# Nyström attention and a gated MLP on one core: the first phase's transposes, sums, landmarks, v load and w3 loads become tokens of the order string, all orders are revised, and the dummy matmuls start sooner

## The chip, the core and the metric

The kernel runs on one core of a Trainium2 chip. The metric is the device time of one execution in microseconds (us), from the first to the last of it. Most executions of one kernel agree closely on one chip; some are longer, most of these at a lower granted TensorE clock (of the kernel before on one chip, 276.58 us at 0.997 of the full clock and 284.16 at 0.978). A run is called slow when it is over 1.5% above the fastest of the same kernel, and only fast runs are compared. TensorE is called PE, VectorE DVE, ScalarE ACT, GpSimd POOL and SyncE SP in the profile.

## The reference, cut to what matters

```python
B, H, S, D = 8, 8, 576, 64          # q, k, v: fp32, 1152 KB per batch and tensor
q_lm, k_lm = means of 18 neighbouring rows of q, k        # 32 landmarks
A  = softmax(q @ k_lm.T / 8);  Bm = softmax(q_lm @ k_lm.T / 8);  C = softmax(q_lm @ k.T / 8)
Z  = Bm.T / (norm1(Bm) * norminf(Bm));  six times: Z = 2*Z - Z @ Bm @ Z
x  = A @ Z @ C @ v                                        # 4608 rows of 512
out = ((x @ w1) * (x @ w2)) @ w3 @ w_out                  # d_ff = 1024, out 4608 x 512
```

## The kernel before

The kernel folds `w3 @ w_out` into one matrix `w34` while the attention of the first batch runs. Everything is scheduled by hand: strings of one-letter tokens give the order in which pieces are issued, and each engine executes its own instructions in that order. Letters that the argument needs:

- `f`: one unit of the fold, three 512-column matmuls (0.647 us); some are preceded by four transposes of a row block of w3. There are 64 of them.
- `C`, `S`, `B`, `T`, `N`, `R`, `P`, `D`, `J`, `X`, `M`, `I`, `Z`, `G`: stages of one batch's attention. `V` multiplies by v, `A` makes scores, `D` the denominators, `I` an inverse step.
- `u`: an "up" unit of the MLP (eight matmuls, 288 columns), `d` and `db`: half of a "down" unit in one or another PSUM bank.
- `p`: a quarter of the v load of a later batch, `t`: a DMA transpose of a quarter of a later batch's q and k, `s` and `h`: GpSimd's group sums and landmarks, `w`: a load of a w3 row block.

`START` is the end of the first phase, `FIRST` the period that begins with batch 0's first `u`, then `ODD` and `EVEN` alternate, and `LAST` is batch 7.

```python
    def load_v(st, b):
        vt = st["vt"] if "vt" in st else pin.tile([128, H, 384], FP32, name="vt")
        nc.sync.dma_start(out=vt[0:NP], in_=v[b].rearrange("h (p r) d -> p h (r d)", p=NP))
        st["vt"] = vt
    # [...]
    def load_weight(t, w):             # wup: two loads of 512 KB for each of w1, w2, on GpSimd's queue
        for qd in range(2):
            nc.gpsimd.dma_start(out=wup[64 * qd:64 * qd + 64, :, t, :],
                                in_=w[256 * qd:256 * qd + 256, :].rearrange("(h d) j -> d h j", d=D))
    # [...]
    def transposes(st, t, hs):         # token t
        # [...]
        nc.sync.dma_start_transpose(out=..., in_=st["qkn"][0:NP, t, hs[0]:hs[0] + n, :]...)

    def turn_on_pe(st, t, h0, copy):   # batch 0: q and k are turned by PE instead
        # [...] 12 PE transposes into a `big` bank, then one copy to qkT

    def sums(st, t, pieces=iter(())):  # four GpSimd adds, about 4.7 us
        # [...]
    # ---- the preamble, in program order ----
        load_qk(sts[0], 0)
        load_qk(sts[1], 1)
        load_weight(0, moe_w1)
        load_weight(1, moe_w2)
        fd = fold(pw, wof, w3f, wsp, warm_up)
        # [...] 16 fold units
        w3f[4] = pf.tile([128, DF], FP32, name="w3f", bufs=3)
        nc.gpsimd.tensor_copy(out=w3f[4][0:NP, 0:1], in_=sts[0]["qkn"][0:NP, 0, 0, 0:1])   # gate: waits for q
        load_w3(4)
        sts[0]["vt"] = pin.tile([128, H, 384], FP32, name="vt")
        nc.gpsimd.tensor_copy(out=sts[0]["vt"][0:NP, 0, 0:1], in_=sts[0]["qkn"][0:NP, 1, 0, 0:1])  # gate: waits for k
        load_v(sts[0], 0)
        turn_on_pe(sts[0], 0, 0, nc.scalar.copy)
        turn_on_pe(sts[0], 0, 4, nc.vector.tensor_copy)
        sums(sts[0], 0)
        # [...] 5 f, k's two turns, w3 block 5, 2 f, landmarks, sums of k, 2 f
        load_w3(6)
        turn_all(1)                    # all four DMA transposes of batch 1, on SP's queue
        steps(fd, 5)
        run(START)
```

A gate is a one-element GpSimd copy into the tile that a load will fill. The load must wait for it, so it cannot be issued before the tensor that the gate reads has landed.

The softmax here doesn't subtract the row's maximum and nothing guards it: scores larger than these inputs give would overflow.

Of the kernel before, what the change touches and what calls it, by code (L numbers as in the profile page):

```python
# [7 lines left out]
FP32 = mybir.dt.float32  # L8
# [5 lines left out]
B = 8  # L14
# [17 lines left out]
def kernel(  # L32
# [12 lines left out]
    START = ("C0 f f h f h f S0 C1 B f w T f f N V0 f S1 A1 f A0 R D P V1 f J0 I0 p f J1 J2 "  # L45
             "I1 f f f f f f f X s I2 p f I3 f f f p I4 f M0 I5 h f s t Z M1 f h f G0 G1 t h "
             "f f G2 p h G3 p f f C0 C1 f f ")
    FIRST = ("u t t u u p S0 u p B u u V0 T A1 N u A0 P R u u f S1 u s D V1 I0 u I1 J1 I2 J0 "
             "u s u h I3 f J2 u X I4 h u u M0 d I5 M1 p Z h d t t h G0 G1 p d C0 G2 C1 G3 d ")
    EVEN = ("u t u S0 u d B p t u p T N V0 A1 u u R u s db S1 u u V1 A0 u I0 D d J0 t P I1 "  # L50
            "J1 u u I2 J2 u s X db I3 u u I4 M0 I5 t M1 u Z db h h G0 h G1 db d h C0 p d G2 "
            "G3 C1 p ")
    ODD = ("u t S0 t p u B p u A1 T N V0 d R s u u S1 u u u d A0 V1 P u I0 u D I1 u J2 s "
           "J0 d I2 u h h u p I3 J1 u u I4 d u I5 h db X db t M1 db M0 t Z db G0 G1 p C0 d "
           "G2 G3 C1 h d ")
    LAST = ("u d u u u db u u d u u db u u u u u u u u d db db db db db db db d d ")
# [474 lines left out]
    for t in qbds:  # L531
        nc.vector.memset(t, 0.0)
# [6 lines left out]
    def steps(g, n=1):  # L539
        for _ in range(n):  # L540
            next(g, None)
# [8 lines left out]
    def all_sums():  # L550
        for b in range(1, B):
            pieces = qk_pieces(sts[b + 1], b + 1) if b + 1 < B else iter(())
            for t in (0, 1):
                sums(sts[b], t, pieces=pieces)
                yield

    def all_landmarks():
        for b in range(B):
            for t in (0, 1):
                for parity in (0, 1):  # L560
                    if b or t:
                        landmarks(sts[b], t, parity)
                        yield

    def all_turns():
        for b in range(2, B):
            for t in (0, 1):
                for h0 in (0, 4):
                    transposes(sts[b], t, range(h0, h0 + 4))
                    yield  # L570

# [20 lines left out]
    queues = dict(p=loads_v(), s=all_sums(), h=all_landmarks(), t=all_turns(), u=all_ups())  # L592

    def run(names):
        for t in names.split():
# [4 lines left out]
            elif t == "w":  # L600
                load_w3(7)
# [12 lines left out]
    with tc.tile_pool(name="pf", bufs=2) as pf:  # L614
# [14 lines left out]
        nc.vector.memset(warm, 0.0)  # L629
        load_w3(0, 0)  # L630
# [16 lines left out]
        warm_up(7)  # L647
# [15 lines left out]
        w3f[4] = pf.tile([128, DF], FP32, name="w3f", bufs=3)  # L663
        nc.gpsimd.tensor_copy(out=w3f[4][0:NP, 0:1], in_=sts[0]["qkn"][0:NP, 0, 0, 0:1])
        load_w3(4)
        sts[0]["vt"] = pin.tile([128, H, 384], FP32, name="vt")
        nc.gpsimd.tensor_copy(out=sts[0]["vt"][0:NP, 0, 0:1], in_=sts[0]["qkn"][0:NP, 1, 0, 0:1])
        load_v(sts[0], 0)
        turn_on_pe(sts[0], 0, 0, nc.scalar.copy)
        turn_on_pe(sts[0], 0, 4, nc.vector.tensor_copy)  # L670
        sums(sts[0], 0)
        steps(fd, 5)
        turn_on_pe(sts[0], 1, 0, nc.scalar.copy)
        turn_on_pe(sts[0], 1, 4, nc.vector.tensor_copy)
        load_w3(5)
        steps(fd, 2)
        landmarks(sts[0], 0, 0)
        landmarks(sts[0], 0, 1)
        sums(sts[0], 1)
        steps(fd, 2)  # L680
        load_w3(6)
        turn_all(1)
        steps(fd, 5)
# [40 lines left out]
```

## Time and profile before

| | before |
|---|---|
| time, median of four runs (us) | 276.66 (275.98 to 277.29) |
| span of the profiled run (us) | 274.0, granted clock 0.999 |
| first transposes of q / first `V` / first `u` start at (us) | 19.79 / 39.90 / 69.04 |
| first period, `FIRST` (us) | 24.54 |
| one `ODD` and one `EVEN` (us) | 52.31 |

The prediction below shows the page, the chain and the waits. One more view: the DMA view of the stretch from 8 to 60 us. Its columns are the load, the issuing queue, the number of issues, the size of each and the median time from issue to landing:

```profile
wup<-in_moe_w_dram POOLq DMA_DIRECT2D x4, 512.0 KB, 30.3
vt<-in_v_dram SPq DMA_DIRECT2D x1, 1152.0 KB, 14.2
```

What matters here is that the first v load takes 14.2 us and that 2 MB of weights (as they are written, in fp16; in HBM they are 4 MB of fp32, the figure that one expectation below gives) are under way on another queue for about 30 us. The weights are issued from 14.3 us on and the last lands at 49.67; they are not needed before `G0` at 62.4 us.

### The profile page before, as it was taken

The numbers are of one execution on the slowest core, as the hardware profiler recorded it, in microseconds if no ns is written. First come the engines' busy times: TensorE is split into PE (matmuls) and PEld (weight loads), VectorE is DVE, ScalarE is ACT, GpSimd is POOL, SyncE is SP. The second block draws the span as 40 slices with busy tenths as digits, with TensorE's granted clock in tenths as the row PEclk, the third lists the DMA queues.
The fourth block names the chain that finished last, engine by engine and source line by source line (L and its number), as shares of the span: only waits on it lengthen the run. The fifth ranks groups of instructions, "written<-read, shape, count | busy, mean of one in ns | idle before, by whom it ended". The sixth has DMA issues, their size and how long they took to land.

```text
span 274.0 us, 9325 instructions
## 1 busy us (share of the span) xinstructions
PE 263.2 (96%) x3874; PEld 148.6 (54%) x3874; DVE 150.8 (55%) x380; ACT 144.0 (53%) x276; POOL 171.0 (62%) x237
## 2 busy tenths in 40 slices
PE   7999989999989999999999999999999999999993
PEld 3546555454654465456545654665465556555642
DVE  5633215464558467545865575559365655674420
ACT  4644445227625855486357455743855476435531
POOL 6446882299699979765996994779879635000000
PEclk9999999999999999999999999999999999999999
DMA  6999999999968999999899899989994231113224
GB/s 211 354 214 248 243 290 151 150 261 128 213 121 142 170 195 218 179 215 201 128 133 259 173 162 188 217 176 156 134 259 130 83 79 42 41 42 79 77 70 122
DMA packets 62138, 45.56 MB, mean 166 GB/s; under 512 B 35600, under 2 KB 54288, under 8 KB 62096
## 3 DMA queue, kind: packets, MB, share of 16 engines
q1 hardware_dynamic: 47488, 32.22, 54.3%
q0 software_dynamic: 13824, 11.54, 30.0%
q10 hardware_dynamic: 784, 1.21, 1.5%
q8 instruction: 30, 0.49, 0.8%
q14 instruction: 12, 0.10, 0.1%
HBM read 38.80 MB, written 9.44 MB: 176 GB/s over the span
## 4 chain that ended last, share of the span: by engine, by line
PE 83%; POOL 6%; DVE 3%; issue 3%; ACT 2%; DVEq 0%; POOLq 0%
PE big L428 24%; PE acc L469 12%; PE acc L508 9%; PE big L469 8%; PE big L377 6%; PE small L321 5%; PE big L411 4%; PE big L495 2%; DVE ab L434 2%; PE small L508 2%; PE big L228 2%; PE big L645 2%; PE big L293 1%; PE big L362 1%; POOL tr L193 1%
## 5 line engine op out<-in xcount | busy, mean ns | idle before, releaser
L428 PE MATMUL big<-ahat,gt 128*128 128x288 f16 x512 | 76.6, 287 | 0.8 <-ACT gt L415 0.5
L434 DVE TENSOR_TENSOR ab<-a_sb,big 128x576 f16<-128x576 f16 x64 | 48.1, 752 | 29.9 <-PE big L428 16.3
L432 ACT CAST a_sb<-big 128x576 f16<-128x576 f32 x64 | 40.8, 638 | 42.8 <-PE big L428 42.7
L428 PEld LDWEIGHTS <-gt 128*128 128x128 f16 x512 | 46.4, 100 | 18.9 <-issue 1.5
L469 PE MATMUL acc<-w,ab 128*128 128x512 f16 x184 | 47.0, 380 | 0.0
L469 PEld LDWEIGHTS <-ab 128*128 128x128 f16 x280 | 24.8, 98 | 25.5 <-issue 3.3
L508 PE MATMUL acc<-wsp,w3t 128*128 128x512 f16 x144 | 35.4, 380 | 0.0
L417 DVE TENSOR_SCALAR gt<-big 128x1024 f16<-128x1024 f32 x16 | 19.6, 1224 | 24.0 <-PE big L411 24.0
L192 POOL TENSOR_TENSOR tr<-qkT 128x768 f32<-128x768 f16 x16 | 26.2, 1637 | 7.6 <-DMA qkT<-qkn 7.5
L508 PEld LDWEIGHTS <-w3t 128*128 128x128 f16 x192 | 17.9, 98 | 18.0 <-issue 0.9
L193 POOL TENSOR_TENSOR tr<-tr,qkT 128x768 f32<-128x768 f32 x16 | 26.3, 1641 | 1.3
L236 POOL TENSOR_TENSOR t<-ect 96x384 f32<-96x384 f32 x16 | 15.9, 995 | 16.1 <-ACT ect L232 14.1
L469 PE MATMUL big<-w,ab 128*128 128x512 f16 x96 | 23.5, 380 | 0.0
L501 DVE SCALAR_TENSOR_TENSOR w3t<-big,w3t 128x512 f16<-128x512 f32 x16 | 11.0, 689 | 18.5 <-ACT w3t L500 18.5
L377 PE MATMUL big<-sz,tz 32*32 32x96 f32 (+1 forms) x768 | 19.2, 248 | 1.7 <-DVE sz L384 1.4
L473 ACT ACTIVATE o_sb<-acc 128x512 f32<-128x512 f32 x23 | 13.7, 597 | 9.7 <-PE acc L469 9.3
L415 ACT ACTIVATE gt<-big 128x1024 f16<-128x1024 f32 x16 | 16.3, 1022 | 3.5 <-PE big L411 3.4
L377 PEld LDWEIGHTS big<-sz,tz 32*32 32x32 f32 x768 | 9.0, 103 | 15.5 <-issue 10.7
L411 PE MATMUL big<-wup,zt 64*32 64x512 f16 x512 | 17.1, 379 | 0.0
L211 ACT COPY far<-o 64x256 f32<-64x256 f32 x32 | 12.9, 403 | 7.9 <-POOL o L197 7.1
L382 DVE TENSOR_TENSOR tz<-big,eye 128x64 f32<-128x64 f32 x40 | 8.8, 221 | 12.7 <-PE big L377 12.2
L500 ACT ACTIVATE w3t<-big 128x512 f16<-128x512 f32 x16 | 9.5, 596 | 11.5 <-PE big L495 11.4
(105 smaller groups left out, 373.4 us busy)
## 6 DMA issues: line engine op xcount, KB each, us to landing
vt<-in_v_dram SPq DMA_DIRECT2D x28, 288.0 KB, 4.5
out_dram<-o_sb SPq DMA_DIRECT2D x23, 192.0 KB, 2.7
qkn<-in_q_dram POOLq DMA_DIRECT2D x12, 288.0 KB, 5.1
qkn<-in_k_dram POOLq DMA_DIRECT2D x12, 288.0 KB, 6.5
w3f<-in_moe_w_dram SPq DMA_DIRECT2D x6, 512.0 KB, 6.6
out_dram<-o_sb SPq DMA_DIRECT2D x24, 128.0 KB, 3.6
wup<-in_moe_w_dram POOLq DMA_DIRECT2D x4, 512.0 KB, 30.3
out_dram<-o_sb SPq DMA_DIRECT2D x23, 64.0 KB, 2.6
```

The costliest lines, as they stand in the source:

```text
L192: nc.gpsimd.tensor_tensor(out=tr, in0=x[:, :, 0, :], in1=x[:, :, 1, :], op=ALU.add)
L193: nc.gpsimd.tensor_tensor(out=tr, in0=tr, in1=x[:, :, 2, :], op=ALU.add)
L236: nc.gpsimd.tensor_tensor(out=t3[0:NP], in0=e[:, :, 0:3, :], in1=e[:, :, 3:6, :], op=ALU.add)
L377: nc.tensor.matmul(psI[32 * t:32 * t + 32, qd, o:96], tz[sl, qd, :], sz[sl, qd, o:96], start=True, stop=True, tile_position=(32 * h, 32 * t))
L411: nc.tensor.matmul(psG[32 * h:32 * h + 32, qd, :], zt[rs, i, h, :], wup[rs, h, w, fs], start=(i == 0), stop=(i == 1), tile_position=(64 * ...
L415: nc.scalar.activation(out=g[:, :, w, fs], in_=psG, func=AXF.Copy, scale=1.0 / ZS)
L417: nc.vector.tensor_scalar(out=g[:, :, w, fs], in0=psG, scalar1=1.0 / ZS, scalar2=None, op0=ALU.mult)
L428: nc.tensor.matmul(p[:, c, 0:HS], st["g"][:, qd, w, 128 * j:128 * j + 128], st["ahat"][qd][:, c, :], start=(qd == 0), stop=(qd == 1))
L432: nc.scalar.copy(out=st["a_sb"], in_=p[:, :, 0:HS])
L434: nc.vector.tensor_tensor(out=st["ab"][:, j, st["t0"]:st["t0"] + S].rearrange("p (c s) -> p c s", c=2), in0=st["a_sb"], in1=p[:, :, 0:HS], ...
L469: nc.tensor.matmul(pso[:, :], ab[:, j, t0:t0 + 128], w34[:, j, :], start=(j == 0), stop=(j == 7))
L508: nc.tensor.matmul(psW[j][:, :], turned[j, c // 4][:, a, c % 4, :], wsp[:, b, c, :], start=(c == 0 and a + b == 0), stop=(c == 7 and a == 1))
```

## The change

It moves the rest of the first phase's hand-written sequence into `START` as tokens, with `x` (PE transposes of q and k), `v` (first v load) and `w` (w3 row blocks), so that each can stand anywhere among the fold units. The other orders are revised, and the memset of the dummy matmuls' operand goes ahead of two others so that the dummies begin sooner. The intent is fewer waits on PE.

```diff
-    START = ("C0 f f h f h f S0 C1 B f w T f f N V0 f S1 A1 f A0 R D P V1 f J0 I0 p f J1 J2 "
-             "I1 f f f f f f f X s I2 p f I3 f f f p I4 f M0 I5 h f s t Z M1 f h f G0 G1 t h "
-             "f f G2 p h G3 p f f C0 C1 f f ")
+    START = ("w x x s f v x f w x h h f f f f f f t t s f f f C0 f w f f h f f f f t S0 h p "
+             "C1 B f f T A0 V0 A1 f N S1 f t f R f D V1 w P J0 f I0 f J2 J1 f X f f f I1 s f "
+             "f I2 p f I3 f f h t I4 f p f I5 M0 f Z s h t f f G0 G1 G2 f C0 G3 h f h p M1 "
+             "C1 f f t f ")
 # [... FIRST, EVEN, ODD, LAST revised as well ...]
-    for t in qbds:
-        nc.vector.memset(t, 0.0)
 # [... sums, landmarks and DMA transposes of the first batches join their queues ...]
+    def first_v():
+        sts[0]["vt"] = pin.tile([128, H, 384], FP32, name="vt")
+        nc.gpsimd.tensor_copy(out=sts[0]["vt"][0:NP, 0, 0:1], in_=sts[0]["qkn"][0:NP, 1, 0, 0:1])
+        load_v(sts[0], 0)
+        yield
 # [... first_turns (x) and loads_w3 (w) likewise ...]
         nc.vector.memset(warm, 0.0)
+        for t in qbds:
+            nc.vector.memset(t, 0.0)
-        warm_up(7)
+        warm_up(8)
 # [... the preamble from load_w3(4) to run(START) goes, see above ...]
```

In `START` the token `s` (GpSimd's sums of q) now stands ahead of `v`, whose gate runs on GpSimd too. Two `t` stand ahead of the third `w`.

More of the change, by code (lines that the diff above doesn't have):

```diff
@@ L44 @@
     nc = tc.nc
-    START = ("C0 f f h f h f S0 C1 B f w T f f N V0 f S1 A1 f A0 R D P V1 f J0 I0 p f J1 J2 "
-             "I1 f f f f f f f X s I2 p f I3 f f f p I4 f M0 I5 h f s t Z M1 f h f G0 G1 t h "
-             "f f G2 p h G3 p f f C0 C1 f f ")
-    FIRST = ("u t t u u p S0 u p B u u V0 T A1 N u A0 P R u u f S1 u s D V1 I0 u I1 J1 I2 J0 "
-             "u s u h I3 f J2 u X I4 h u u M0 d I5 M1 p Z h d t t h G0 G1 p d C0 G2 C1 G3 d ")
-    EVEN = ("u t u S0 u d B p t u p T N V0 A1 u u R u s db S1 u u V1 A0 u I0 D d J0 t P I1 "
-            "J1 u u I2 J2 u s X db I3 u u I4 M0 I5 t M1 u Z db h h G0 h G1 db d h C0 p d G2 "
-            "G3 C1 p ")
-    ODD = ("u t S0 t p u B p u A1 T N V0 d R s u u S1 u u u d A0 V1 P u I0 u D I1 u J2 s "
-           "J0 d I2 u h h u p I3 J1 u u I4 d u I5 h db X db t M1 db M0 t Z db G0 G1 p C0 d "
-           "G2 G3 C1 h d ")
-    LAST = ("u d u u u db u u d u u db u u u u u u u u d db db db db db db db d d ")
+    START = ("w x x s f v x f w x h h f f f f f f t t s f f f C0 f w f f h f f f f t S0 h p "
+             "C1 B f f T A0 V0 A1 f N S1 f t f R f D V1 w P J0 f I0 f J2 J1 f X f f f I1 s f "
+             "f I2 p f I3 f f h t I4 f p f I5 M0 f Z s h t f f G0 G1 G2 f C0 G3 h f h p M1 "
+             "C1 f f t f ")
+    FIRST = ("u u p S0 u t u B p p u A1 V0 A0 T N u P f R u u f s S1 u u D V1 I0 u J1 I1 f "
+             "J0 s I2 u h u h J2 I3 u X I4 u u M0 I5 d M1 Z h d t G0 h G1 d p C0 t t G2 C1 "
+             "G3 db ")
+    EVEN = ("u S0 u t B u u T V0 A1 u N u u R db u p S1 db A0 V1 p p s u I0 t P D u J0 u I1 "
+            "J1 d u I2 db J2 X u I3 u u s I4 M0 I5 h h M1 u Z db h G0 t h G1 db C0 d p G2 t "
+            "G3 C1 db ")
+    ODD = ("p u S0 t u B A1 p T u p V0 N d R u u S1 s u u d u A0 V1 u I0 D J2 u u I1 J0 d "
+           "s I2 P h u u I3 h J1 u u I4 t h d I5 u db X t t d d Z M0 d M1 G0 p G1 C0 d G2 "
+           "G3 C1 h db ")
+    LAST = ("u u d u u u d u u u d u u u u d u u u u d d db d db db db db db d ")
     consts = ctx.enter_context(tc.tile_pool(name="consts", bufs=1))
@@ L550, in all_sums @@
     def all_sums():
-        for b in range(1, B):
-            pieces = qk_pieces(sts[b + 1], b + 1) if b + 1 < B else iter(())
+        for b in range(B):
+            pieces = qk_pieces(sts[b + 1], b + 1) if 0 < b < B - 1 else iter(())
             for t in (0, 1):
@@ L560, in all_landmarks @@
                 for parity in (0, 1):
-                    if b or t:
-                        landmarks(sts[b], t, parity)
-                        yield
+                    landmarks(sts[b], t, parity)
+                    yield
     def all_turns():
-        for b in range(2, B):
+        for b in range(1, B):
             for t in (0, 1):
@@ L570, in all_turns, with first_turns, loads_w3 @@
                     yield
+    def first_turns():
+        for t in (0, 1):
+            turn_on_pe(sts[0], t, 0, nc.scalar.copy)
+            yield
+            turn_on_pe(sts[0], t, 4, nc.vector.tensor_copy)
+            yield
+    def first_v():
+        sts[0]["vt"] = pin.tile([128, H, 384], FP32, name="vt")
+        nc.gpsimd.tensor_copy(out=sts[0]["vt"][0:NP, 0, 0:1], in_=sts[0]["qkn"][0:NP, 1, 0, 0:1])
+        load_v(sts[0], 0)
+        yield
+    def loads_w3():
+        w3f[4] = pf.tile([128, DF], FP32, name="w3f", bufs=3)
+        nc.gpsimd.tensor_copy(out=w3f[4][0:NP, 0:1], in_=sts[0]["qkn"][0:NP, 0, 0, 0:1])
+        for j in range(4, 8):
+            load_w3(j)
+            yield
     waiting = []
@@ L591 @@
     atts, done = [], {}
-    queues = dict(p=loads_v(), s=all_sums(), h=all_landmarks(), t=all_turns(), u=all_ups())
+    queues = dict(x=first_turns(), v=first_v(), w=loads_w3(), p=loads_v(), s=all_sums(), h=all_landmarks(), t=all_turns(), u=all_ups())
     def run(names):
@@ L599, in run @@
                 steps(fd)
-            elif t == "w":
-                load_w3(7)
             elif t[0] == "d":
@@ L662 @@
         steps(fd, 8)
-        w3f[4] = pf.tile([128, DF], FP32, name="w3f", bufs=3)
-        nc.gpsimd.tensor_copy(out=w3f[4][0:NP, 0:1], in_=sts[0]["qkn"][0:NP, 0, 0, 0:1])
-        load_w3(4)
-        sts[0]["vt"] = pin.tile([128, H, 384], FP32, name="vt")
-        nc.gpsimd.tensor_copy(out=sts[0]["vt"][0:NP, 0, 0:1], in_=sts[0]["qkn"][0:NP, 1, 0, 0:1])
-        load_v(sts[0], 0)
-        turn_on_pe(sts[0], 0, 0, nc.scalar.copy)
-        turn_on_pe(sts[0], 0, 4, nc.vector.tensor_copy)
-        sums(sts[0], 0)
-        steps(fd, 5)
-        turn_on_pe(sts[0], 1, 0, nc.scalar.copy)
-        turn_on_pe(sts[0], 1, 4, nc.vector.tensor_copy)
-        load_w3(5)
-        steps(fd, 2)
-        landmarks(sts[0], 0, 0)
-        landmarks(sts[0], 0, 1)
-        sums(sts[0], 1)
-        steps(fd, 2)
-        load_w3(6)
-        turn_all(1)
-        steps(fd, 5)
         run(START)
```

## The prediction

> **What bounds the kernel now.** I read the page first, then the chain of waits, then the waits of TensorE, then the timeline and DMA view of the first 70 us.
>
> The page's first part:
> ```profile
> PE 263.2 (96%) x3874; PEld 148.6 (54%) x3874; DVE 150.8 (55%) x380; ACT 144.0 (53%) x276; POOL 171.0 (62%) x237
> ```
> TensorE is the bound; nothing else passes 62%. But 263.2 us of 274.0 does not mean that only 10.8 us are idle: matmul ends are modelled. The chain of waits shows the true rate, because each piece there ends where the next begins:
> ```profile
> 69.20 1.47 PE big L428 x12
> ...
> 96.99 0.97 PE acc L469 x4
> ...
> 99.42 1.49 PE big L428 x12
> 100.91 0.86 PE acc L469 x4
> ```
> Twelve 288-column matmuls take 1.47 us (122.5 ns each), four 512-column ones 0.86 us (216 ns). So I measured PE by start-to-start intervals in the trace, unit by unit (a unit is one letter of the order strings), and called excess over the shortest interval of the same unit before the same kind of successor a stall. The 0.97 of the third line is no stall: the unit after it uses smaller PE tiles, and that costs about 93 ns, every time.
>
> All stalls together come to 9.9 us. Where the chain leaves PE, they show:
> ```profile
> 20.04 2.71 issue
> 22.95 1.60 POOL tr L192
> 24.62 1.66 POOL tr L193
> ...
> 34.94 0.96 POOL t L236
> ...
> 43.45 0.66 ACT eat L299
> ...
> 143.59 0.66 issue
> 145.00 1.03 ACT gt L415
> ```
> ```profile
> PE big L377 <- DVE sz L384: 1.4, 4, 0.7
> PE small L333 <- POOL es L241: 0.8, 1, 0.8
> PE big L428 <- ACT gt L415: 0.5, 2, 0.2
> PE small L341 <- ACT eat L299: 0.5, 1, 0.5
> PE big L133 <- DMA qkn<-in_q_dram: 0.4, 1, 0.4
> ```
> By part of the program: first phase (up to 69.0 us) 3.2 us, of it 0.44 the cold clock beside the second group of dummies, 0.60 before the first transposes of q at 19.79 (the q load lands at 19.75), 0.92 + 0.10 at S0 at 36.9 (a POOL chain from 22.75: sums, landmarks, second sums, row sums), 0.14 + 0.55 at the denominators at 44.1, 0.35 at two adjacent inverse steps, the rest crumbs. FIRST (69.0 to 93.6) 2.4 us, mostly two adjacent inverse steps (0.77), V1 directly ahead of I0 (0.51), M0 directly behind u61/u70 (0.41). Each EVEN+ODD pair is exactly 52.30 us and holds about 1.36 us: 0.43 at the turn from EVEN to ODD (the first up waits for a bank of `big` that G2's eviction holds), 0.12 at B, about 0.17 twice where a unit waits for an ab product, 0.30 at I5, 0.09 behind M1, 0.10 at S0. LAST 0.2.
>
> **What the Trainium skill says.** "TensorEngine Tiling (Array Packing)", Tiling Modes, Key Properties: changing the tiling mode drains TensorE. The trace agrees: 956 against 863 ns for the same four matmuls, so 93 ns. "Perfetto Trace Analysis", Tensor Engine Instruction: the end of a matmul in a profile is estimated from its size; hence starts only. "DMA: Bandwidth & Descriptors", Queues, rings and completion order: SP has one ring on each DMA engine, consumed in ring order, and an engine takes turns between the queues that have work. The trace agrees with both halves, as the timeline shows:
> ```profile
> 22.98 0.33 SPq L89 DMA_DIRECT2D vt<-in_v_dram  x1
> 23.41 5.49 SPq L622 DMA_DIRECT2D w3f<-in_moe_w_dram  x2
> ...
> 28.99 15.94 SPq L122 DMA_TRANSPOSE qkT<-qkn  x2
> ```
> The v load lands at 37.2, the w3 row blocks 5 and 6 behind it at 39.91 and 42.41; the two transposes block SP's issue for 15.94 us and land at 50.19 and 52.77, just as the weights of the other queue (wup, landing to 49.67) are in. What stands behind a DMA transpose in SP's order is late.
>
> **The change, part by part.**
>
> 1. Dummies sooner, eight for seven. The memset of `warm` goes ahead of two qbd memsets (0.55 us), so PE should start near 1.2 for 1.75 us, and the eighth dummy (0.427 us cold) fills that. The first transposes wait for a load at about 4.75 and the first q transposes for a load at 19.75, issued when other loads land. PE already waited 0.60 us there. Gain at 19.79: nothing, the wait gets longer.
>
> 2. First phase reordered. Static PE work does not change: by the program order, 227 changes of tiling mode before, 228 after. I summed the measured unit intervals over both orders: 252.98 before, 253.30 after, so +0.3 us. What moves is waits.
>  - Between q's and k's transposes stand now one fold unit with its transposes (1.08 us) instead of five. PE gets to k's at about 21.9; k lands at 22.72: a new stall, +0.85.
>  - The POOL sums no longer stand behind the gate for v (which waited for k until 22.77): they start at about 21.8 for 22.91. S0 now has seven fold units and two transposes (5.4 us) between it and C0, against 3.56 needed: 1.02 gained. R, D and all I's are separated by fold units: 0.14 + 0.55 + 0.35 gained. Sum −2.06.
>  - The price: the gate for v stands behind the sums on POOL, so v is issued at about 26.7 for 22.98. The queue had only one other piece ahead of it before, so I estimate landing at 38.5 to 40.5. V0 comes at 38.4 + 0.85 = 39.2: 0 to 1.3 stalled. w3's row block 6 (the third w token) now stands behind two DMA transposes in SP's order. In the old order those issued until 44.9; in the new one I estimate that the block lands at 50 to 53, and the unit that transposes it comes at 48.5 + 0.85 + V0's stall, about 49.9. So 0 to 3 stalled, middle 1.5. Together about +2.0, the least certain number here.
>  Net of the first phase: −2.06 + 0.85 + 2.0 = +0.8 (from −1.2 to +3).
>
> 3. FIRST. I1 and I2 are no longer adjacent (−0.77), M0 still stands behind u71, V1 still directly ahead of I0 (0.5 stays), new waits of about 0.1 each at u61, u71, I4, I5. −1.1.
>
> 4. EVEN and ODD. The second half of a down unit (0.86 us, in a bank it already holds) now stands between C1 and the next period's first up: 0.43 + 0.10 gone, twice (EVEN6 leads into LAST, which had no wait). B's 0.12 gone three times, because the down unit ahead of it moves. "I4 M0 I5 M1 u Z" stays, so 0.17 + 0.30 + 0.09 remain. Per pair 52.3 to about 51.65; in sum −1.4.
>
> 5. LAST: downs spread among ups, the 0.2 before the first down goes; the tail of 4.4 us behind the last matmul stays. −0.2.
>
> Sum: +0.3 + 0.8 − 1.1 − 1.4 − 0.2 = −1.6 us. With the first phase's middle guess at its worse half already in, I shift by −1 because a tuned order more probably avoids the late block than not: −2.6, so 276.6 − 2.6 = 274.0.
>
> **The rivals.**
>  - First rival: the first phase is clean (v and w3 land in time; only the k stall stays). For it: in the old order the queue idles little, and a load moved later leaves its share to others. Then the first phase gives −1.2 and the whole −3.6: about 273.0, and at best 271.5 if FIRST's waits go entirely.
>  - Second rival: SP's order takes the gain back. Transposes that took 10.63 and 5.3 us to issue stand ahead of a w3 block; POOL and DMA work is the same and only later. The first phase loses 3 to 4 us, periods give 2.7: 277.
>  - Third rival: POOL (41.4 of each 52.3 us) becomes the bound where landmarks and sums moved. Against it: 79% busy, with PE waits on it only at S0. It would give 276.
>
> **Range and chances.** The floor from PE is 274.0 − 9.9 + 0.3 = 264.4 span with no stall at all, and half of the stalls by my count cannot go with these orders. 271.05 or less (2%) needs nearly all of parts 2 to 5 with no new wait: 0.08. Over 282.1 needs over 8 us of new waits: 0.02. Range 271.6 to 276.9.
>
> **What would show it.** k's transposes waiting for the load of k until 22.7; the first dummy at 1.2 but q's transposes still at 19.8; S0 and the denominators without a wait; V0 and the transposes of w3's block 6 with or without a DMA wait; an EVEN+ODD pair near 51.65 us; no wait of the up for gt; still 0.3 at I5 in EVEN. It is wrong if the q transposes come well before 19.7, if pairs stay at 52.3, or if new PE waits on DMA pass 4 us.

## The result, and the profile after

The changed kernel takes 279.25 us (median of four fast runs, 279.19 to 280.42) against 276.66. Ratios in this document are the mean time of one kernel's fast runs over the mean time of the other's fast runs of the same rounds on the same chip, so they are not quite the ratios of the medians. Here the ratio is 1.0104, with a 95% interval of 1.0068 to 1.014. The result lies within 2%, but it is a loss of about 1%, and the prediction (274.0, at most 276.9) missed it.

| start (us) | before | after | difference |
|---|---|---|---|
| first transposes of q | 19.79 | 20.19 | +0.40 |
| PE ready for the first `V` | 39.90 | 39.65 | −0.25 |
| first `V` | 39.90 | 43.94 | +4.04 |
| first `u` of batch 0 | 69.04 | 74.00 | +4.96 |
| first `u` of batch 1 | 93.58 | 98.69 | +5.11 |
| first `u` of batch 3 | 146.07 | 150.60 | +4.53 |
| first `u` of batch 5 | 198.38 | 202.28 | +3.90 |
| end | 274.03 | 277.42 | +3.39 |

So all of the loss is in the first phase, and everything after it gains 4.96 − 3.39 = 1.57 us. The new `START` also holds one fold unit (0.65 us) fewer than the old first phase and `FIRST` one more. For the same work the first phase loses 4.96 + 0.65 = 5.6 us and the rest gains 1.57 + 0.65 = 2.2 us.

TensorE's waits in the changed kernel (line and tile that waited, what released it, total, times, longest) answer to the waits shown of before:

```profile
PE small L323 <- DMA vt<-in_v_dram: 4.2, 1, 4.2
PE big L135 <- DMA qkn<-in_q_dram: 1.3, 1, 1.3
...
PE big L379 <- DVE sz L386: 0.7, 3, 0.2
PE big L135 <- DMA qkn<-in_k_dram: 0.6, 1, 0.6
```

The waits at `S0` (`small` on `es`) and at the denominators (`small` on `eat`) are gone, and so is that of the first `u` on `gt`, as predicted. The wait on the load of k is the predicted one. The new wait is that of `V0` for v, 4.2 us. The chain of waits, followed back from there, shows why v comes late:

```profile
22.33 1.64 POOL tr L194
...
27.27 0.14 POOL vt L580
...
27.43 16.37 DMA vt<-in_v_dram
...
43.94 1.51 PE small L323 x48
```

The gate of v (`vt` on POOL) stands behind the four sums, so v is issued at 27.43 instead of 22.98. It then takes 16.37 us, although less stands ahead of it on its queue. The DMA view of the same stretch as before:

```profile
wup<-in_moe_w_dram POOLq DMA_DIRECT2D x4, 512.0 KB, 24.2
...
vt<-in_v_dram SPq DMA_DIRECT2D x1, 1152.0 KB, 16.4
```

The weights land sooner than before (the last at 45.83 instead of 49.67), and v slower. Last, the clock. The page's line of the granted clock in 40 slices, and the busy time by stretch (start and end, length, then busy time and instructions of PE, PEld, DVE, ACT and POOL, then the granted clock, DMA share and GB/s):

```profile
PEclk9999995999999999999999999999999999999999
```
```profile
39.40:43.90 4.50, 0.32 (x9) 0.11 (x8) 1.27 (x6) 0.65 (x1) 2.05 (x5) 0.76 1.32 270
43.90:50.00 6.10, 6.06 (x87) 3.92 (x87) 0.86 (x2) 1.56 (x3) 0.00 (x0) 0.61 1.07 229
50.00:73.50 23.50, 23.50 (x352) 11.97 (x338) 12.23 (x27) 10.97 (x21) 16.72 (x21) 1.00 0.87 152
```

PE stands still for most of the first stretch, and in the 6.1 us after the wait it runs at a granted clock of 0.61. I compared each unit there with the same unit at full clock: `V0`, `A1`, `f`, `S1`, the transposes behind it, and the units to 50 us are 0.63, 0.12, 0.61, 0.15, 0.45 and 0.21 us too long, 2.2 us in sum. The clock record of this profile says it more finely: half the full clock from 41.78 to 48.61, so from 2.1 us after PE's last matmul until 4.67 us after the wait. Half of 4.67 is 2.3 us. So one late load seems to cost 4.2 us of waiting and 2.2 us of slow work after it. The experiments test both, and what made the load late.

### The profile page after: what moved, and what is told of

It reads as the page before. It is cut to its first block, busy times and chain, and to the rows that moved or that the text cites. A ratio compares the mean times of both kernels' runs of the same rounds, so it can differ in the third digit from the quotient of the medians.

```text
span 277.4 us, 9334 instructions
## 1 busy us (share of the span) xinstructions
PE 263.2 (95%) x3875; PEld 148.5 (54%) x3875; DVE 150.9 (54%) x380; ACT 143.8 (52%) x276; POOL 171.1 (62%) x237
## 4 chain that ended last, share of the span: by engine, by line
PE 78%; DMA 13%; DVE 3%; POOL 3%; issue 1%; ACT 1%; POOLq 0%; DVEq 0%
PE big L430 23%; PE acc L471 15%; PE big L471 8%; PE acc L510 7%; DMA vt<-in_v_dram 6%; PE big L413 5%; PE big L379 5%; PE small L323 5%; DMA wof<-in_moe_w_out_dram 3%; DMA qkn<-in_q_dram 3%; PE big L230 2%; DVE ab L436 2%; PE big L364 1%; PE big L295 1%; PE big L497 1%
## 5 line engine op out<-in xcount | busy, mean ns | idle before, releaser
L436 DVE TENSOR_TENSOR ab<-a_sb,big 128x576 f16<-128x576 f16 x64 | 48.2, 753 | 26.2 <-ACT a_sb L434 14.1
L510 PE MATMUL acc<-wsp,w3t 128*128 128x512 f16 x144 | 37.1, 386 | 0.3 <-DVE wsp L491 0.3
L323 PE MATMUL small<-vt,ect 96*32 96x64 f32 x768 | 14.6, 226 | 4.2 <-DMA vt<-in_v_dram 4.2
```

The costliest lines, as they stand in the source:

```text
L323: nc.tensor.matmul(psV[32 * h:32 * h + 32, 0:64], ects[qd][0:NP, h, r, :], st["vt"][0:NP, 4 * qd + h, 64 * r:64 * r + 64], start=(r == 0), ...
L436: nc.vector.tensor_tensor(out=st["ab"][:, j, st["t0"]:st["t0"] + S].rearrange("p (c s) -> p c s", c=2), in0=st["a_sb"], in1=p[:, :, 0:HS], ...
L510: nc.tensor.matmul(psW[j][:, :], turned[j, c // 4][:, a, c % 4, :], wsp[:, b, c, :], start=(c == 0 and a + b == 0), stop=(c == 7 and a == 1))
```

## The experiments

Three theories were set against each other. **A**: the first v load and what stands behind it lose the DMA engines to the wup weights, so that any load that the new order issues later than the old one is late. **B**: the position of the gate on GpSimd alone is to blame; put v where it was, and the predicted gain appears. **C**: the new periods lose something as well. Beside them stands the question whether the clock's fall is a cost of its own. "Before" on the same chip varied between 276.7 and 277.9 in median, with slow runs up to 284, so ratios count for more than times. As a second measure I take the time from the first transposes of q to the first `u`, because the landing of q varied from 17.6 to 21.2 us between runs; in before it is 69.04 − 19.79 = 49.25, in the changed kernel 74.00 − 20.19 = 53.81. (For equal work add 0.65 us to a kernel with the new `START`.)

### First set: what of the change does what

**The v token ahead of the sums**

```diff
-    START = ("w x x s f v x f w x ...
+    START = ("w x x v s f x f w x ...
```

> The changed kernel with the v token moved ahead of the first sums, so that GpSimd's gate copy for v stands before them again. Theory (late v: its gate behind the sums issues v at 27.43 instead of about 23.2, V0 waits 4.2 us and the idle time drops the PE clock, about 2.2 us more): v issued near 23.2, landing 37.5 to 39.5, V0 at about 39.7 with under 0.5 us of wait, granted clock back to 0.999, time 279.25 - 6.2 = about 273.0. The sums start at about 23.3 instead of 22.33, which may cost up to 0.5 at S0 or S1. Rival (SP's order: two DMA transposes stand ahead of w3's block 6, as the prediction feared): the wait only moves from V0 to the transposes of w3's blocks 5 or 6, and the time stays at 277 to 279.

Measured: 278.92 us in median (275.51 to 280.9, one slow run), ratio 1.0016 (0.992 to 1.011). In the profile, which fell on the fastest run, v is issued at 21.08, lands at 34.07 and `V0` doesn't wait. But the next load in SP's order is late instead:

```profile
PE big L497 <- DMA w3f<-in_moe_w_dram: 2.9, 1, 2.9
```

Two DMA transposes hold SP's issue for 17.67 us, and the w3 row block behind them is issued at 43.50 and lands at 50.66. After this wait of 2.9 us the clock is at half for 3.4 us as well. From q to the first `u` it is 51.6 us. B's promise isn't kept: the wait moves from v to w3, which the prediction had counted among its least certain numbers.

**The gate of v on ScalarE**

```diff
-        nc.gpsimd.tensor_copy(out=sts[0]["vt"][0:NP, 0, 0:1], in_=sts[0]["qkn"][0:NP, 1, 0, 0:1])
+        nc.scalar.copy(out=sts[0]["vt"][0:NP, 0, 0:1], in_=sts[0]["qkn"][0:NP, 1, 0, 0:1])
```

> The changed kernel with its token order kept, but the one-element gate copy that holds the v load back until k has landed is on ScalarE instead of GpSimd. Theory (it is only GpSimd's queue that delays v): v issued at about 23.5 although its token still stands behind the sums; the sums keep their early start at 22.3; no wait at V0 above 0.5 us; about 272.8, a little better than the version with the token moved. Rival (loads of v and w3 share one ring and the DMA transposes stand in it): a new PE wait of 1 to 3 us on w3's block 5 or 6, 275 to 277.

Measured: 280.25 us (279.21 to 282.2), ratio 1.0109 (1.003 to 1.019). v is issued at 23.04, as in before, lands at 38.34, and `V0` has no wait. The same w3 block now waits 4.8 us:

```profile
27.18 20.48 SPq L124 DMA_TRANSPOSE qkT<-qkn  x2
47.77 0.73 SPq L639 DMA_DIRECT2D w3f<-in_moe_w_dram  x1
```

These lines are of SP's queue (start, length of the issue, instruction). The two transposes take 20.48 us to issue, and the block behind them lands at 54.04. B falls with this run: v early, and the loss is all there.

**The new periods with the old first phase**

```diff
-             "f f G2 p h G3 p f f C0 C1 f f ")
+             "f f G2 p h G3 t f f C0 C1 f f ")
 # and FIRST, EVEN, ODD, LAST of the changed kernel; nothing else
```

> The kernel before with its own first phase, and the changed kernel's FIRST, EVEN, ODD and LAST orders alone (one p of START is turned into a t so that the queues stand where the new orders expect them; nothing wrong in the result). Theory (the periods gained what was predicted and the first phase lost it all): the EVEN and ODD pair at 51.7 us for 52.3, first up at about 69.0, time 276.6 - 2.0 = about 274.5. Rival (the revised periods are themselves no better, or the slow start brings them their gain): within 0.5 us of the kernel before, 276.2 to 277.

Measured: 274.75 us (273.94 to 277.04), ratio 0.992 (0.986 to 0.998). In the mean of the fast runs the periods alone gain about 2 us (the interval leaves 0.5 to 4). The profile doesn't show that gain: from the first `u` to the end it takes 205.02 us, and before took 204.99. A pair (batch 3 to batch 5) takes 52.24 us, not the expected 51.7, and `FIRST` takes 25.48 us instead of 24.54. The run isn't the periods alone, either: the old `START` leaves only two fold units, so the third `f` of the new `FIRST` does nothing, I1 and I2 stand next to each other again, and PE waits 0.7 us there, as in before. `S0` of batch 1 waits 0.6 us for POOL as well. The changed kernel has neither wait. So it is the changed kernel's own profile that speaks against theory C, with 2.2 us less behind the first `u` for equal work; this run agrees in its times only.

**The wait for v filled with 18 dummy matmuls**

```diff
-             "C1 B f f T A0 V0 A1 f N ...
+             "C1 B f f T A0 # V0 A1 f N ...
+            elif t == "#":
+                keep_warm(18)          # 18 matmuls of 512 columns into a free bank
```

> The changed kernel with 18 dummy matmuls of 512 columns (18 x 0.216 = 3.9 us) put between A0 and V0, inside the time that PE waits for v; v is as late as before. Theory (the idle 4.2 us drop PE's clock and cost about 2.2 us more after the wait): V0 starts at 43.9 as before, granted clock back to about 0.999, the units behind it at full speed, time 279.25 - 2.2 = about 277.0. Rival (the units behind V0 are slow because DMA traffic or other engines hold them up, not the clock): no change, 279.2, or slower by what the dummies overrun.

Measured: 278.02 us (277.34 to 278.68), ratio 1.0025 (0.9985 to 1.0064). The dummies end after v is in, so `V0` comes 0.46 us later than in the changed kernel, at 44.40. Yet the first `u` comes 1.67 us sooner, at 72.33. From `V0` to the first `u` it is 27.93 us against 30.06. The busy time by stretch, to be set beside the changed kernel's:

```profile
44.40:50.00 5.60, 5.60 (x147) 3.57 (x146) 1.08 (x3) 2.10 (x4) 1.10 (x3) 1.00 1.01 204
```

The clock stays at 1.00. So the fall of the clock is a cost of its own of 30.06 − 27.93 = 2.1 us, and it is paid only because PE stood idle for 4.2 us before.

### Second set: both loads early, and lateness by itself

**The gate on ScalarE and the third w3 load ahead of the two transposes**

```diff
-    START = ("w x x s f v x f w x h h f f f f f f t t s f f f C0 f w f f h ...
+    START = ("w x x s f v x f w x h h f f f f f f w t t s f f f C0 f f f h ...
 # and nc.scalar.copy for the gate of v, as above
```

> The version with v's gate on ScalarE, and the third w token (w3's block 6) moved ahead of the two t tokens, so that no DMA transpose stands before that load on SP. Theory (two late loads, one behind the other: while V0 waits for v, block 6 has time to land; with v early, block 6 itself is what PE waits for, 4.8 us in the run with the gate on ScalarE, because two transposes take until 47.8 to issue): no PE wait on DMA above 0.5 us except the q and k loads at the first transposes; granted clock 0.999; first up near 68; span about 271.5, time about 273.5, 1.0 to 1.5% under the kernel before. Rival (DMA is simply full there, and each load moved ahead makes another one late): a new wait of 2 us or more on w3's block 5 or 7, on the DMA transposes of batch 1, or on wup; 276 or more.

Measured: 278.96 us (275.59 to 281.61, one slow run), ratio 1.0012 (0.995 to 1.007). In the profile (275.6, at the fast end) neither v nor row block 6 waits. Two other waits stand in their place, TensorE's waits again:

```profile
PE big L230 <- POOL qbd L214: 2.0, 1, 2.0
PE big L497 <- DMA w3f<-in_moe_w_dram: 1.6, 1, 1.6
```

The second is w3 row block 7, now the one behind transposes. The first is `C0` of batch 1 on its q landmarks. The chain shows where that comes from:

```profile
28.95 9.61 SPq L124
...
38.61 13.13 DMA qkT<-qkn
...
52.24 1.64 POOL tr L194
...
65.34 0.73 POOL qbd L214
66.11 0.51 PE big L230 x12
```

The first of batch 1's transposes holds SP's issue for 9.6 us, and the second lands 13.1 us after its own issue. From 52.2 GpSimd needs about 14 us of sums and landmarks, and then `C0` of batch 1 may start, at 66.11. In before, too, POOL's first sum of batch 1 started at 52.91 and its q landmarks ended at 66.75, just ahead of `C0` at 67.19. So there was 0.4 us of slack in before: **the transposes' landing is a second bound of the first phase**, and with the landing as it was, removing PE's waits ahead of it could gain little more than that.

**Both moves by tokens alone, with the gate on GpSimd**

```diff
-    START = ("w x x s f v x f w x h h f f f f f f t t s f f f C0 f w f f h ...
+    START = ("w x x v s f x f w x h h f f f f f f w t t s f f f C0 f f f h ...
```

> The changed kernel with nothing but two tokens moved: v ahead of the first sums (gate still on GpSimd) and w3's block 6 ahead of the two t tokens. Theory: as with the gate on ScalarE, up to 0.5 us slower because the sums start some 0.8 us later: about 273.8. If the wait on block 6 stays although it stands ahead of the transposes, the theory on SP's order is wrong: then about 278 as in the version with v alone moved.

Measured: 278.76 us (277.65 to 279.69), ratio 1.0035 (0.9975 to 1.0095). PE waits 2.3 us for q, 1.8 for w3 block 7 and 1.8 at `C0` of batch 1. It agrees with the run before it: where the gate stands makes no difference that these runs can tell once the load is early.

**The transposes of k three fold units later**

```diff
-    START = ("w x x s f v x f w x h h f f f f f f w t t ...
+    START = ("w x x s f v f f x w x h h f f f f f w t t ...
```

> As the version with both loads early, and the first k transposes stand three fold units behind the q transposes instead of two tokens' worth (one unit). Theory (PE gets to k's transposes 0.6 to 0.8 us before the load of k is in): that wait goes, 0.5 to 0.8 us better than with both loads early, about 272.8. Rival (the wait only hides a later one, S0 or the clock of loads): no difference.

Measured: 277.53 us (274.67 to 279.85, two slow runs), ratio 0.9958 (0.988 to 1.0035). The wait for k is gone, but those for w3 block 7 (2.3) and at `C0` (1.6) take its place. From q to the first `u` it is 51.2 us against 51.0 of the run with both loads early: nothing won. A wait that stands ahead of another bound can be free, which would fit.

**Before, with the v load alone made late**

```diff
 # in the kernel before: gate and load of v moved behind the turns of q and the sums
         turn_on_pe(sts[0], 0, 4, nc.vector.tensor_copy)
         sums(sts[0], 0)
+        sts[0]["vt"] = pin.tile([128, H, 384], FP32, name="vt")
+        nc.gpsimd.tensor_copy(out=sts[0]["vt"][0:NP, 0, 0:1], in_=sts[0]["qkn"][0:NP, 1, 0, 0:1])
+        load_v(sts[0], 0)
```

> The kernel before, with one part of the change alone: v's gate and load stand behind the first q transposes and sums, as in the changed kernel; all else is untouched. Theory: v issued near 27.3, landing near 43; V0, which PE reaches at 39.5, waits 3 to 4 us, and the clock falls: 3 to 5.5 us slower than before, about 280 to 282. Rival (the wait at V0 is nothing but the first phase's new order, with PE being there sooner): under 1 us slower.

Measured: 283.18 us (280.86 to 285.8, one slow run), ratio 1.0168 (1.009 to 1.024). v is issued at 26.81 and lands at 43.12, after 16.3 us, as in the changed kernel. A wait of 4.3 us at `V0` and the fall of the clock (0.984 in the mean) follow. So a gate behind the sums is enough to cause the loss in the old order too, while wup is loading: the first `u` comes at 75.37 against 69.04, 6.3 us later, about the 4.2 and 2.1 found above.

### Third set: the weights out of the way

**The periods, with the gate on ScalarE behind the turns of q**

```diff
 # the run "new periods with the old first phase", and gate and load of v behind the turns of q:
+        nc.scalar.copy(out=sts[0]["vt"][0:NP, 0, 0:1], in_=sts[0]["qkn"][0:NP, 1, 0, 0:1])
```

> The periods-alone version (old first phase, new FIRST, EVEN, ODD, LAST), with v's one-element gate copy on ScalarE behind the first q copy instead of on GpSimd ahead of the sums. The DMA order stays as before, v issued at about 23. Theory: the GpSimd sums start about 1 us sooner, the wait of S0 on the row sums (0.4 to 0.9) goes, but the first phase cannot end much sooner, because C0 of batch 1 waits for a chain from the DMA transposes (landing near 52) through 14 us of GpSimd work, which has under 0.5 us of slack in the kernel before. So 0 to 0.5 us better than periods alone, about 274.2 on an undisturbed chip, 1% under the kernel before. Rival (PE's own waits in the first phase set its end): a full 0.9 better.

Measured: 276.05 us (273.16 to 278.62, two slow runs), ratio 0.9893 (0.982 to 0.9965). The interval overlaps that of the periods alone (0.986 to 0.998), and the profile has 2.1 us of waits on w3 row blocks, so it is inconclusive whether the gate helps there.

**Both loads early, and the four wup loads issued at 42 us instead of 14**

```diff
-        load_weight(0, moe_w1)
-        load_weight(1, moe_w2)
-             "C1 B f f T A0 V0 A1 f N ...
+             "C1 B f f T W A0 V0 A1 f N ...
+            elif t == "W":
+                load_weight(0, moe_w1)
+                load_weight(1, moe_w2)
 # on top of the run with both loads early
```

> The version with both loads early, and the four wup loads (4 MB, needed from 60 us on) issued by GpSimd at about 40 us instead of 14 us. Theory (the first phase is bound by DMA: wup takes turns with v, w3 and the transposes of batch 1, whose results then start a 14 us GpSimd chain to C0 of batch 1): transposes landing by about 45 instead of 51.7, no wait on w3's block 7 (1.6) nor of C0 on qbd (2.0), first up 2.5 to 3.5 us sooner than with both loads early, at 66.5 to 68; if wup lands by 60, time about 271.5 on an undisturbed chip. Rival (transposes are slow by themselves, not for wup): they land near 50 as before and nothing is won; wup then lands late and G0 waits.

Measured: 272.33 us (271.27 to 273.17, six fast runs), ratio 0.9828 (0.978 to 0.987). The four DMA transposes land at 39.0 to 44.5 instead of 50 to 55, and wup lands at 50.6 to 58.2, still ahead of `G0`. Of DMA waits on PE, only these are left:

```profile
PE big L135 <- DMA qkn<-in_q_dram: 1.8, 1, 1.8
...
PE big L135 <- DMA qkn<-in_k_dram: 0.7, 1, 0.7
```

The first phase takes 47.4 us from q, 1.8 fewer than before and 3.6 fewer than with both loads early.

**Both loads early, and batch 1's q landmarks ahead of its k sums**

```diff
-             "f I2 p f I3 f f h t I4 f p f I5 M0 f Z s h t f f ...
+             "f I2 p f I3 f f h t I4 h f p f I5 M0 f Z s t f f ...
```

> The version with both loads early, and the second landmark token of batch 1's q stands ahead of the sums of its k instead of behind them, so that qbd is complete at about 60 instead of 66. Theory (C0 of batch 1 waits 2.0 us for qbd because GpSimd works in order): that wait is gone, the one on w3's block 7 (1.6) stays, 2 us better than with both loads early: first up near 68.5. Rival: C0's wait moves to S0 of batch 1 or to the DMA, less than 1 us is won.

Measured: 277.74 us (276.48 to 279.62), ratio 1.0031 (0.998 to 1.008). The wait of `C0` on `qbd` is gone, but PE waits 2.2 us for w3 block 7 and slow units follow (0.44, 0.68 and 0.26 us too long, with the clock at half from 59.25 to 62.66). Nothing is won: GpSimd's chain isn't what costs the time while the loads are late.

**All of these together**

```diff
 # k later + both loads early + wup at 42 us + landmarks ahead
+    START = ("w x x s f v f f x w x h h f f f f f w t t s f f f C0 f f f h f f f f t S0 h p "
+             "C1 B f f T W A0 V0 A1 f N S1 f t f R f D V1 w P J0 f I0 f J2 J1 f X f f f I1 s f "
+             "f I2 p f I3 f f h t I4 h f p f I5 M0 f Z s t f f G0 G1 G2 f C0 G3 h f h p M1 C1 f f t f ")
```

> All that helped together on the changed kernel: v's gate on ScalarE, w3's block 6 ahead of the transposes, k's transposes later, wup issued at 40 us, landmarks ahead of the k sums. Theory: no wait over 0.5 us in the first phase but those of the clock and the q load; first up near 67; span about 270.5, time about 272.3 on an undisturbed chip, 1.5 to 2% under the kernel before. Rival: DMA as a whole is full to about 60 us, so that wup or block 7 takes the place: 274 to 276.

Measured: 272.61 us (271.2 to 274.45), ratio 0.9842 (0.979 to 0.989), 47.0 us from q to the first `u`. On the same chip as the version with only wup and both loads moved, it isn't better.

### Fourth set: is it wup, or the late issue?

Four more kernels were run because the set before had moved loads and weights together.

**The changed kernel, with only wup moved**

```diff
-        load_weight(0, moe_w1)
-        load_weight(1, moe_w2)
-             "C1 B f f T A0 V0 A1 f N ...
+             "C1 B f f T W A0 V0 A1 f N ...
 # the gate of v stays behind the sums, the third w behind two t
```

> The changed kernel with nothing altered but the four wup loads, issued at about 42 us instead of 14. Theory A (contention with wup is the cause; the late issue hurts only under it): v, issued at 27.4, lands near 37, no wait at V0, transposes by 40, block 6 without a wait; time within 0.5 us of the version with both loads early and wup later, 272 to 272.8. Theory B (the late issue alone is enough): V0 still waits 2 us or more and the clock falls: 275 to 277.

Measured: 272.98 us (271.91 to 274.63, six fast runs), ratio 0.9894 (0.984 to 0.995). v is issued as late as in the changed kernel, at 27.21. The DMA view of the same stretch, from 8 to 60 us:

```profile
wup<-in_moe_w_dram POOLq DMA_DIRECT2D x4, 512.0 KB, 10.5
...
vt<-in_v_dram SPq DMA_DIRECT2D x1, 1152.0 KB, 8.2
```

It takes 8.2 us instead of 16.4, lands at 35.40, and `V0` comes at 39.43 without a wait. SP's two transposes hold its issue for half as long as well, and the w3 block behind them is issued 9 us sooner; PE waits 0.2 us for w3 in this profile. Changed kernel first, then this run, SP's queue:

```profile
28.43 17.33 SPq L124 DMA_TRANSPOSE qkT<-qkn  x2
45.86 0.53 SPq L639 DMA_DIRECT2D w3f<-in_moe_w_dram  x1
```
```profile
28.22 8.32 SPq L124 DMA_TRANSPOSE qkT<-qkn  x2
36.64 0.53 SPq L642 DMA_DIRECT2D w3f<-in_moe_w_dram  x1
```

This decides between A and B: with the gate exactly where the change put it, the loss is gone. The first `u` comes at 67.36 (74.00 in the changed kernel). The profiled span is 271.7 against 277.4; 1 us of the gain is given back in a period where a `d` waits 0.8 us for the eviction of `o_sb`.

**Before, with wup moved; and the periods, with wup moved**

```diff
-    START = ("C0 f f h f h f S0 C1 B f w T f f N V0 ...
+    START = ("C0 f f h f h f S0 C1 B f w T W f f N V0 ...
 # load_weight moved to W as above; the second run has the new periods as well
```

> The kernel before with nothing altered but wup's issue (about 42 us instead of 14). If its first phase is held by the chain from the DMA transposes to C0 of batch 1 (under 0.5 us of slack) but its PE order has its own waits, wup later alone wins little here: 0 to 1 us, 275.5 to 276.6 on an undisturbed chip, and the new first phase is needed to use the room. Rival: wup alone is worth all of the gain, 2 us or more, and the new first phase nothing.

> The old first phase, the new periods, wup at about 42 us. Periods alone were worth about 2 us; if the old first phase wins nothing from wup, 274.3 here on an undisturbed chip, and the changed kernel with wup later is 1.5 to 2.5 us better, which is then what the new first phase is worth once DMA is out of its way. Rival: the two are equal at about 272.3, and the new first phase is worth nothing.

Measured on the same chip: 275.21 us (273.68 to 278.34, one slow run), ratio 0.9964 (0.991 to 1.002) for before; 275.17 us (274.16 to 275.71), ratio 0.997 (0.993 to 1.001) with the new periods. Later weights by themselves gain the old order about 1 us (the interval runs from 2.5 us gained to 0.5 lost), and neither ratio is clear of 1. Against these two the changed order with wup later is 2.2 us faster in median, so the new `START` is worth having once the DMA engines are free for it. Where it gains is not quite what the expectation says: for equal work the first phase from q takes 48.0 us in its profile (47.36 + 0.65), against 48.9 and 48.2 in these two. Against the second, which has the same periods, most of the gain stands in `FIRST`, which takes 25.34 us there and 24.69 − 0.65 = 24.04 for equal work behind the new `START`: the third `f` is missing again, and PE waits 0.7 us between I1 and I2 and 0.4 us at `S0`. These waits explain part of why the new periods gain nothing beside later weights here. The rest is open: one pair of periods, batch 2 to batch 4, took 53.0 us, where other runs with these orders had anything from 51.7 to 52.8.

**Before, with sooner dummies alone**

```diff
-    for t in qbds:
-        nc.vector.memset(t, 0.0)
         nc.vector.memset(warm, 0.0)
+        for t in qbds:
+            nc.vector.memset(t, 0.0)
-        warm_up(7)
+        warm_up(8)
```

> The kernel before with the sooner dummies alone (memset of warm ahead of qbd's, eight for seven). The prediction's step: PE starts at 1.2 for 1.75, reaches the q transposes about 0.3 to 0.5 sooner and waits longer for the q load: no gain, within 0.3 us of before. Rival: the fold's transposes and products run warm sooner and the whole chain moves: 0.5 us better.

Measured: 277.31 us (275.69 to 279.66), ratio 1.005 (0.998 to 1.012), unclear. In the profile q landed at 20.84 and PE waited 2.2 us for it, with units too long after that (0.8, 0.44 and 0.43 us; the clock was at half from 21.02 to 24.43). Starting sooner didn't bring q sooner; whether it makes q later stays open, because q's landing also varied in kernels that don't differ there. There is a hint: in the twelve profiles with the sooner dummies q landed at 20.1 us in the mean (17.95 to 21.17), in the six others at 19.2 (17.61 to 19.75). They are single runs on several chips, so nothing is shown.

### All runs side by side

| run | ratio to before (95%) | q to first `u` (us) |
|---|---|---|
| changed | 1.0104 (1.0068–1.014) | 53.8 |
| v before the sums | 1.0016 (0.992–1.011) | 51.6 |
| v's gate on ScalarE | 1.0109 (1.003–1.019) | 55.0 |
| new periods alone | 0.992 (0.986–0.998) | 48.7 |
| changed, wait filled | 1.0025 (0.9985–1.0064) | 51.4 |
| both loads early | 1.0012 (0.995–1.007) | 51.0 |
| both loads early, by tokens alone | 1.0035 (0.9975–1.0095) | 51.8 |
| both loads early, k later | 0.9958 (0.988–1.0035) | 51.2 |
| before, v late | 1.0168 (1.009–1.024) | 55.8 |
| new periods, gate on ScalarE | 0.9893 (0.982–0.9965) | 50.5 |
| both loads early, wup later | **0.9828 (0.978–0.987)** | 47.4 |
| both loads early, landmarks ahead | 1.0031 (0.998–1.008) | 51.1 |
| all together | 0.9842 (0.979–0.989) | 47.0 |
| changed, wup later | 0.9894 (0.984–0.995) | 47.4 |
| before, wup later | 0.9964 (0.991–1.002) | 48.9 |
| new periods, wup later | 0.997 (0.993–1.001) | 48.2 |
| before, sooner dummies | 1.005 (0.998–1.012) | 50.9 |
| before | 1 | 49.25 |

The lowest is the changed kernel with v's gate on ScalarE, the third w3 load ahead of the transposes and wup at 42 us: 272.33 us, 1.7% under before; "all together" isn't told apart from it. Whether the first two of these add anything to the third isn't shown: the runs with and without them were on different chips, and from q to the first `u` they take the same time.

## Why the prediction was wrong, point by point

- **The landing of v (wrong, the step that failed).** The prediction put the gate behind the sums and the issue at 26.7, and it was 27.43. Then it said "The queue had only one other piece ahead of it before, so I estimate landing at 38.5 to 40.5", which leaves about 12 to 14 us for the load. It measured 16.37. Even the 14.2 us of the profile of before would have given 27.43 + 14.2 = 41.6 and a wait of 2 us. The premise was that SP's own queue made the load long. The prediction had itself cited that a DMA engine takes turns between the queues that have work, and its trace had the sign of it: the weights, issued from 14.3, landed only from 39.33 on, behind v, which was issued at 22.98 and landed at 37.20. It didn't use that for v. The run with only wup moved shows the real cause: the same load, just as late in the same queue, took 8.2 us without the weights on the other queue. So the term "0 to 1.3 stalled" was 4.2.
- **A missing term, the clock (wrong by omission).** The prediction counted a wait as its length. The fall of the clock cost another 2.1 to 2.2 us behind it, as the filled wait showed.
- **w3 behind two transposes (mechanism right, put in the wrong place).** The predicted 1.5 us measured 0.15 in the changed kernel, because the wait for v hid it. When v was made early, it appeared at once: 2.9 and 4.8 us. v and w3 together were put at +2.0 and measured 4.2 + 0.15 + 2.2 = 6.6.
- **The waits removed (right).** `S0`, denominators and adjacent inverse steps of the first phase no longer wait. The wait for k measured 0.79 from start to start (0.6 in the view of waits, which leaves out the time to notice) for a predicted 0.85. But the time that those removals free could not all be won even with early loads, since the transposes of batch 1 bound the first phase with 0.4 us of slack. The prediction had no such floor.
- **Sooner dummies (right).** No gain was predicted and none was found.
- **FIRST (half right).** −1.1 predicted; 24.54 with two fold units became 24.69 with three, which is −0.5 for equal work.
- **EVEN and ODD (right).** 51.65 predicted for a pair, 51.68 measured (batch 3 to batch 5), and the turn from one period to the next has no wait.
- **The rivals.** The second, "SP's order takes the gain back", 277, was nearest in time, but in the changed kernel PE waited only 0.15 us for what stood behind the transposes; that wait came only in the experiments. The third, GpSimd as the bound, has no wait of PE on POOL to show for it in the changed kernel's list. The first, a clean first phase and "about 273.0", is what the changed kernel does when wup is moved: 272.98. Its first phase is then 67.36 + 0.65 − 69.04 = −1.0 us against before, near the −1.2 that this rival gave it.
- **The shift by −1 (wrong).** It rested on the belief that a tuned order avoids late loads. Nothing in the profile carried it, and it went in the wrong direction.
- **The sum of the errors.** The first phase came out at +5.6 for a predicted +1.1 (0.8 and the static 0.3), which is 4.5 us; 4.6 of that is v with the clock and 0.4 a later q, so about 0.5 was better than predicted elsewhere. `FIRST` adds 0.6, the later periods −0.1 (−1.7 for −1.6), the shift 1.0: together 6.0. The profiled run of before was 0.8 us under the median (275.83 and 276.66), which leaves 5.2 of the 5.25 us between 274.0 and 279.25.

Open: why v took 16.4 rather than 14.2 us although less stood ahead of it (the weights landed 3.8 us sooner in that profile, which would fit a larger share for them, but no run separates this); why q lands anywhere from 17.6 to 21.2; and the spread of 4 to 6 us between runs of several of the experiment kernels, which the changed kernel (1.2 us) did not have.

## What to carry to other kernels

Before moving a load later, take its measured duration and ask which transfers on *other* queues run at that time: they, not its own queue, may set it. A large load that is needed last should be issued last; here 2 MB of weights, issued 48 us ahead of their use, held up what was needed sooner. With them issued later the changed order took 0.9894 of before's time, and 1.0104 without (on another chip); in the old order the same move gained 0.4%, which isn't clear of nothing, so it is the order with the DMA engines free for it that pays. And a wait on TensorE can cost more than itself. The four waits of 2.9 to 4.8 us in the first phase of these profiles were each followed by 3.4 to 6.8 us at half clock (in part inside the wait), and so were two of six between 2.0 and 2.3 us; dummies in the gap buy that part back.

## What the Trainium skill lacked or had wrong

- "TensorE: Matmul & The Clock Gate", What's actually happening: it gives about 3.4 us for the window of idleness that throttles and about 3.4 us of activity that releases. The traces agree in kind, with half the clock in pieces of 3.41 or 6.83 us, but less idleness was enough: in the 4.2 us wait the clock fell 2.1 us after the last matmul, and it also fell with waits of 2.16 and 2.25 us in all (and not with others of 2.26 and 2.31). That section gives no price for one such gap; the page's later one on oscillation works one out for gaps that come back at every step of a loop. Here a single gap cost 2.1 to 2.2 us on top of the 4.2, and 18 dummy matmuls in it kept the clock at 1.00 and saved 2.1 us.
- "DMA: Bandwidth & Descriptors", Queues, rings and completion order and DMA Transpose (X-bar): these sections give no figure for what a load or a transpose on SP's queue loses to loads on GpSimd's queue. Here the same 1152 KB took 16.4 us beside 2 MB of weights and 8.2 without, and two DMA transposes held SP's issue for 17.3 us beside them and 8.3 without; whatever stood behind them waited as long.
- "TensorEngine Tiling (Array Packing)", Tiling Modes, Key Properties: it says that changing the mode drains TensorE and gives no figure. Here one change costs 93 ns (956 against 863 ns for the same four matmuls), and the program has 227 of them.
